# Linear attention followed by an MLP mixer on one core: loads of one batch placed anew, small matmuls regrouped, u transposed by slabs, and the last tile split

## The chip, the core and the metric

The kernel runs on one core of a Trainium2 chip. The time is the device time in microseconds of one execution; before the change it was 253.14 us (median of three runs, 253.03 to 253.78). The profile is of one more execution, with a span of 251.7 us.

## The reference

```python
# q, k, v: (8 batches, 8 heads, 576 positions, 64), float32; phi(x) = elu(x) + 1
kv  = einsum('bhsd,bhse->bhde', phi(k), v);  z = sum(phi(k), axis=2)
x   = (phi(q) @ kv) / (phi(q) . z + 1e-6)         # heads side by side: (8, 576, 512)
u   = x + (relu(x^T @ w_tok1) @ w_tok2)^T         # tokens: 576 -> 256 -> 576
out = u + relu(u @ w_ch1) @ w_ch2                 # channels: 512 -> 1536 -> 512
```

## The kernel before, in words

**Tiling.** Each batch has 576 positions: four tiles of 128 and a tail of 64. The tails of two batches (0 and 1, 2 and 3, ...) are put together into one tile of 128, `ut`. Matmuls are in bf16 and accumulate in eight PSUM banks.

**Stages of one batch n.** `load` (L126) brings q, k and v in halves c = 0 and 1 from SyncE's queue into `raw`; batch 1 has buffers of its own, all others share one set. `phi_exp` (ScalarE), `phi_add` and `phi_end` (VectorE, L151 to L164) make phi of k and q; `vcast` (L171) casts v to `vs` in halves, which `kv` (L181) multiplies with phi(k) in 64x64 tiles of TensorE, half 0 and then half 1; two ScalarE copies (L194) put the result into `kvbd`. `qtr_dma` (L216) transposes phi(q) by DMA. `nd` or `nd_all` (L249) multiplies by `kvbd` and divides: that is x. `mm1` (L296) and `mm2` (L307) are the token MLP and give u; `mm2_tails` (L330) does the tail rows of two batches in 128x64 tiles of TensorE and adds x to them on VectorE (L340), which gives `ut`. u is transposed, by DMA (`utr_dma` L508, `utr_tail_dma` L514) for batches 2 to 7, by TensorE for batches 0 and 1 (`utr_first` L487, `utr` L362), where PSUM is then copied into `uT` by ScalarE and VectorE. `mm3` (L520) is the first channel matmul, twelve groups of four matmuls of 512 columns (`mm3(n, mc, range(0, 2))` does half of a group), with the relu into `cr` on ScalarE or VectorE; `mm3_tail` (L537) is the same for the tails' tile, in three parts.

**The second channel matmul.** For batches 1 to 7 it is done in seven block products (`pair_product` L679, and `product` L629 for batch 7) instead of eight. `row_sums` (L620) prepares their left sides. The products 1, 6, 7 and 4 accumulate onto one bank X in this order, with readings in between: `pair_copy` (ScalarE) and `pair_end` (L699, VectorE adds u; GpSimd then adds a copied part at L703). A product that accumulates onto a bank has to wait until the reading ahead of it is done. The tails' tile goes through `mm4(p, 8, ...)` (L548) in full.

**Order.** It is written out by hand. TensorE runs a list of large pieces `big` (in batch n's block: twelve mm3 groups, three tail groups when n is odd, fourteen products, and the three parts of the tails' tile when n is odd). `fill` is a list of (step, piece) pairs: a piece is emitted after the large piece with that number. In the blocks from batch 2 on (L978 to L1042), `b0` is the step of the first product (12 or 15), and the fill pieces work on batches n+1 and n+2: `nd`, `mm1`, `mm2` and the transposes of u of batch n+1, `phi`, `vcast` and `kv` of batch n+2, loads of batch n+3. Each engine takes its instructions in the order in which they are emitted, SyncE's queue of transfers too. What stands behind a waiting instruction in such a queue waits with it.

**Places that the change touches.** The start of batch 0 (L833 to L840, and `big` at L893); casts and `kv` of batch 1 (`late`, L904); the block of batch 1 (L921 to L976) with `kv` of batch 2 at step 8, `nd` of batch 2 at step 10, `qtr_dma(3)` at step 15, the transposes of u of batch 2 at steps 19 and 24, and all loads of batch 4 (q, v, k) at step 25; the blocks of batches 2 to 6, with `mm2_tails` and its transpose `utt` at step b0 + 6, loads of q and v at b0 + 7, and `kv` and then `pair_end` X at b0 + 9; the order `LAST` (L709) of batch 7.

Of the kernel before, what the change touches and what calls it, by code (L numbers as in the profile page):

```python
# [10 lines left out]
BF16 = mybir.dt.bfloat16  # L11
# [7 lines left out]
def kernel(  # L19
# [20 lines left out]
    nc = tc.nc  # L40
# [5 lines left out]
    R = 4  # L46
# [6 lines left out]
    NDM = DM // 128  # L53
    NCH = DCH // 128
# [10 lines left out]
    def bank(at=None):  # L65
        if at is None:
            at, ring[1] = ring[1], (ring[1] + 1) % 4
        return psum[:, at]
# [6 lines left out]
    def two16():  # L75
        return banks().bitcast(BF16).rearrange("p a (t s) -> p a t s", s=128)


    def const(name, shape, dt=BF16):
        return consts.tile(shape, dt, name=name, tag=name)  # L80
# [17 lines left out]
    u = [const(f"u{b}", [128, R, DM]) for b in range(2)]  # L98
    ut = [const(f"ut{i}", [128, DM]) for i in range(2)]
    uT = [const(f"uT{b}", [128, R, NDM, 128]) for b in range(2)]  # L100
    uTt = const("uTt", [128, NDM, 128])
    cr = [const(f"cr{b}", [128, NCH, SM]) for b in range(2)]
    crt = const("crt", [128, NCH, 128])
# [19 lines left out]
    def rb(n):  # L123
        return 1 if n == 1 else 0
# [46 lines left out]
    def vcast(n, c, copy=nc.scalar.copy):  # L171
        js = slice(2 * c, 2 * c + 2)
        copy(out=vs[:, js, :, 0:D],  # L173
             in_=raw["v", rb(n)][:, js].rearrange("p j (t d) -> p j t d", t=T))
# [187 lines left out]
    def utr(n, js):  # L362
        b = n % 2
        for jp in js:
            tp = bank(4 + 2 * jp).bitcast(BF16).rearrange("p (j r c) -> p j r c", j=2, r=R)
            for i in range(2):
                j = 2 * jp + i
                for r in range(R):
                    nc.tensor.transpose(out=tp[:, i, r, :],
                                        in_=u[b][:, r, 128 * j:128 * j + 128], identity=identity)  # L370
            for i, copy in enumerate((nc.scalar.copy, nc.vector.tensor_copy)):
                copy(out=uT[b][:, :, 2 * jp + i], in_=tp[:, i])

    COLS = [slice(0, DM // 2), slice(DM // 2, DM)]

# [111 lines left out]
    def utr_first(js, put):  # L487
        tp = two16()[:, 0].rearrange(
            "p (j r) c -> p j r c", j=2)[:, 0:len(js)]
        for i, j in enumerate(js):  # L490
            for r in range(R):
                nc.tensor.transpose(out=tp[:, i, r, :],
                                    in_=u[0][:, r, 128 * j:128 * j + 128], identity=identity)
        put(out=uT[0][:, :, js[0]:js[-1] + 1].transpose([0, 2, 1, 3]), in_=tp)

    def w2_put(kt, t0, t1):
        nc.gpsimd.tensor_copy(
# [22 lines left out]
    def mm3(n, mc, kjs=range(NDM), dve=False):  # L520
        b = n % 2
        if kjs[0] == 0:
            part_of[mc] = bank(None if n == 0 else (
                (0, 1, 0, 1, 2, 3, 0, 1, 2, 3, 0, 1) if n > 1 else
                (3, 5, 7, 0, 3, 1, 2, 0, 3, 1, 0, 1))[mc])
        ps = part_of[mc]
        for kj in kjs:
            nc.tensor.matmul(out=ps, lhsT=wc1[:, kj, 128 * mc:128 * mc + 128],  # L528
                             rhs=uT[b][:, :, kj],
                             start=(kj == 0), stop=(kj == NDM - 1))  # L530
        if kjs[-1] == NDM - 1 and dve:
            nc.vector.tensor_scalar(out=cr[b][:, mc, :], in0=ps, scalar1=0.0, scalar2=None,
                                    op0=ALU.max)
        elif kjs[-1] == NDM - 1:
            nc.scalar.activation(out=cr[b][:, mc, :], in_=ps, func=AF.Relu)  # L535
# [169 lines left out]
    def pair_put(n):  # L705
        for e in range(2):
            nc.gpsimd.dma_start(out=outv[n, :, e:e + 7:2], in_=live["o4"][half[e]])

    LAST = [(1, 0), (2, 0), (6, 0), (5, 0), (7, 0), (3, 0), (4, 0), None,  # L709
            (1, 1), (2, 1), (6, 1), (5, 1), (7, 1), (3, 1), (4, 1)]  # L710

    def m4s(n):
        if n + 1 < B:
            return [lambda i=i, j=j: pair_product(n, i, j) for i in ORDER for j in range(2)]
        out_ = []
        for e in LAST:
            out_ += [lambda e=e: product(n, e[1], e[0])] if e else m4(n // 2, [8])
        return out_

    def prep_k(n, g, copy=nc.scalar.copy):  # L720
        phi("k", n, g)
# [69 lines left out]
    dve, act = nc.vector.tensor_copy, nc.scalar.copy  # L791
# [45 lines left out]
        mm3(0, mc, range(0, 2))  # L837
    utr_first([2], act)
    utr_first([3], dve)
    mm3(0, 2, range(0, 2))  # L840

    for nm in "kqv":
        for c in range(2):
# [28 lines left out]
    def run(bigs, fill):  # L872
# [5 lines left out]
        for s, fn in fill:  # L878
# [4 lines left out]
    m4 = lambda p, ts: [lambda t=t, i=i: mm4(p, t, range(4 * i, 4 * i + 4))  # L883
                        for t in ts for i in range(3)]


    def m4_0(kc):
        ts, kcs = (range(2 * kc, 2 * kc + 2), [0, 1]) if kc < 2 else (range(R), [kc])
        for k_ in kcs:
            for t in ts:  # L890
                mm4(0, t, [k_], wait=True)

    big = [lambda mc=mc: mm3(0, mc, range(2, 4)) for mc in range(3)] + \  # L893
        [lambda mc=mc: mm3(0, mc, dve=mc in (3, 6, 9)) for mc in range(3, NCH)] + \
        [lambda kc=kc: m4_0(kc) for kc in range(NCH)]
    at0 = {"qt0": 12, "qt1": 14, "vc": 13, "kv": 14, "nd00": 15, "nd01": 16, "nd10": 17,
           "nd11": 18, "nd20": 19, "nd21": 20, "mm1": 21}
# [1 line left out]
    for ex, ad, en, nm, c in ((2, 2, 3, "k", 0), (5, 5, 6, "k", 1), (8, 8, 9, "q", 0),  # L899
# [1 line left out]
        fill += [(ex, lambda nm=nm, c=c: phi_exp(nm, 1, 2 * c, 2)),  # L901
                 (ad, lambda nm=nm, c=c: phi_add(nm, 1, 2 * c, 2)),
                 (en, lambda nm=nm, c=c: phi_end(nm, 1, 2 * c, 2))]
    late = [("vc", lambda: vcast(1, 0)), ("vc", lambda: vcast(1, 1, nc.vector.tensor_copy))]  # L904
    fill += [(21, lambda g=g: phi("q", 2, g)) for g in range(2)]
    fill += [(22, lambda: qtr_dma(2)), (22, lambda: load_all(3, "q"))]
    fill += [(22, lambda: weight_sums((tf, B12, B11), (tb[1], B22, tf)))]
# [10 lines left out]
    for mc in range(3):  # L918
        mm3(1, mc, range(0, 2))
    utr_tail(0)  # L920
    big = [lambda mc=mc: mm3(1, mc, range(2, 4)) for mc in range(3)] + [  # L921
        lambda mc=mc: mm3(1, mc, dve=mc in (5, 8)) for mc in range(3, NCH)] + [
        lambda i=i: mm3_tail(i, False) for i in range(3)] + m4s(1) + m4(0, [8])
    fill = []
    put = lambda s, fn, *a: fill.append((s, lambda: fn(*a)))
# [11 lines left out]
    put(4, vcast, 2, 0)  # L937
    put(5, vcast, 2, 1, nc.vector.tensor_copy)
    put(6, load_all, 3, "v")
    put(8, kv, 2, range(2))  # L940
    for g in range(2):
        put(9, phi_add, "q", 3, 2 * g, 2)
    put(10, todo["nd"])
# [24 lines left out]
    put(24, pair_end, 1, "Z", 0, 0, 0)  # L968
    put(24, todo["mm2b"])
    put(24, todo["utb"])  # L970
    put(25, load_all, 4, "qvk")
    put(26, pair_end, 1, "Y", 0, 1, 1)
    put(28, pair_end, 1, "X", 1, 0)
    put(28, pair_put, 1)
# [3 lines left out]
    for n in range(2, B - 1):  # L978
        p, b = divmod(n, 2)
        big = m3(n) + (m3t if b else []) + m4s(n) + (m4(p, [8]) if b else [])  # L980
        b0 = 15 if b else 12
        todo = dict(steps(n + 1))
        fill = []
        put = lambda s, fn, *a: fill.append((s, lambda: fn(*a)))
        at = lambda s, *nms: [put(s, todo.pop(nm)) for nm in nms if nm in todo]

        def phi_at(nm, ex, ad, en):
            for g in range(2):
                if ex is not None:
                    put(ex[g], phi_exp, nm, n + 2, 2 * g, 2)  # L990
            for g in range(2):
                put(ad[g], phi_add, nm, n + 2, 2 * g, 2)
                put(en[g], phi_end, nm, n + 2, 2 * g, 2)

        at(1, "nd")
        if n + 2 < B:
            if n > 3:
                phi_at("k", None, (2, 2), (3, 4))
                put(5, load_all, n + 3, "k")
            if n != 3:  # L1000
                phi_at("q", (7, 7), (8, 9), (9, 10))
            else:
                phi_at("k", (7, 7), (8, 9), (9, 10))
            put(10, *((qtr_dma, n + 2) if n != 3 else (load_all, n + 3, "k")))
            if n == 2:
                for g in range(2):
                    put(10, phi_add, "k", n + 2, 2 * g, 2)
        at(7, "mm1")
        for s, k0 in ((11, 0), (12, 3)):
            for w in (1, 2):  # L1010
                put(s, row_sums, n, w, k0, 3)
        if n == 3:
            phi_at("q", (12, 13), (13, 13), (14, 14))
            put(15, qtr_dma, n + 2)
        at(13, "mm2a", "uta")
        put(14, row_sums, n, 3, 0, KH)
        put(b0 + 1, pair_copy, 0)
        if n == 2:
            for g in range(2):
                put(b0 + 1, phi_exp, "k", n + 2, 2 * g, 2)  # L1020
                put(b0 + 2, phi_end, "k", n + 2, 2 * g, 2)
            put(b0 + 4, load_all, n + 3, "k")
        at(b0 + 3 - b, "mm2b", "utb")
        put(b0 + 4 - b, row_sums, n, 4, 0, KH)
        put(b0 + 4 - b, pair_end, n, "Z", 0, 0, 0)
        put(b0 + 5, pair_copy, 1)
        if n + 2 < B:
            for g in range(2):
                put(b0 + (5 if n == 2 else 2) + g, vcast, n + 2, g)
        at(b0 + 6, "mm2t", "utt")  # L1030
        put(b0 + 7, load_all, n + 3, "qv")
        put(b0 + 7, pair_copy, 2)
        if n > 2 and n + 3 < B:
            put(b0 + 8, k_exp, n + 3)
        if n + 2 < B:
            put(b0 + 9, kv, n + 2, range(2))
        put(b0 + 9, pair_end, n, "X", 1, 1, 2)
        put(b0 + 11, pair_end, n, "Y", 0, 1, 1)
        put(b0 + 13, pair_end, n, "X", 1, 0)
        put(b0 + 13, pair_put, n)  # L1040
        assert not todo, todo
        run(big, sorted(fill, key=lambda e: e[0]))  # L1042

    n = B - 1
# [33 lines left out]
```

## Time and profile before

| | |
|---|---|
| median time | 253.14 us |
| span of the profiled run | 251.7 us |
| TensorE matmuls | 240.4 us busy, 2411 |
| VectorE | 171.3 us busy, 296 |
| ScalarE | 141.0 us busy, 224 |
| GpSimd | 68.8 us busy, 80 |
| granted TensorE clock | 0.997 |
| DMA | 48.39 MB, mean 192 GB/s |

A page of the profile has busy times, a strip of 40 slices of the span, the queues of DMA, the chain of work that ended last, and the costliest groups of instructions. A group stands as line, engine, operation, written tile <- read tiles, shape and count. In the timeline each row begins with the start and the duration, both in us, and ends, in brackets, with the idle time of the engine just before and what ended it. Neighbouring instructions of one kind are merged into one row; its count is behind the x. A few matmul records are missing from the trace, so that a count can be one short. "PE" is the matmul side of TensorE, "PEld" its weight load; "SPq" is the queue of SyncE from which transfers are issued.

### The profile page before, as it was taken

How to read it: one execution, taken by the hardware profiler on the slowest of the kernel's cores; microseconds unless marked ns; L12 is line 12 of the kernel's file. 1: busy time of each engine (PE TensorE's matmuls, PEld its weight loads, DVE VectorE, ACT ScalarE, POOL GpSimd, SP SyncE). 2: the span in 40 equal slices, each digit the busy share in tenths (PEclk: the TensorE clock that was granted, in tenths of full speed). 3: DMA queues.
4: the chain of work that ended last, by engine and by line, in shares of the span. 5: the costliest groups of instructions: out<-in, count | busy, mean ns of one | idle time of the engine just before them, and what ended most of it. 6: DMA issues, size and time to landing. Idle time of an engine off the chain costs nothing.

```text
span 251.7 us, 5859 instructions
## 1 busy us (share of the span) xinstructions
PE 240.4 (96%) x2411; PEld 151.6 (60%) x2430; DVE 171.3 (68%) x296; ACT 141.0 (56%) x224; POOL 68.8 (27%) x80
## 2 busy tenths in 40 slices
PE   7699999999999999989999999999999999999993
PEld 3584455554867546754578545774678445764962
DVE  5955777889998466967594397939863444834542
ACT  4764781578774378626896178556863265137300
POOL 9770130496703500061004500250004500260000
PEclk9999999999999999999999999999999999999998
DMA  6999999999534999389938956569142540435034
GB/s 239 261 203 262 347 257 339 322 274 294 233 51 87 227 399 261 69 225 392 348 76 196 393 153 219 120 208 353 45 97 46 112 99 0 83 66 124 0 97 115
DMA packets 49707, 48.39 MB, mean 192 GB/s; under 512 B 30032, under 2 KB 35536, under 8 KB 49680
## 3 DMA queue, kind: packets, MB, share of 16 engines
q1 hardware_dynamic: 41568, 34.87, 46.5%
q0 software_dynamic: 7568, 12.49, 22.0%
q10 hardware_dynamic: 544, 0.66, 1.1%
q8 instruction: 19, 0.31, 0.5%
q14 instruction: 8, 0.07, 0.1%
HBM read 35.85 MB, written 9.44 MB: 180 GB/s over the span
## 4 chain that ended last, share of the span: by engine, by line
PE 76%; DVE 8%; DMA 7%; ACT 4%; issue 2%; SPq 1%; DVEq 0%; ACTq 0%
PE ps L528 25%; PE ps L692 19%; DMA k_raw<-in_k_dram 7%; PE ps L555 6%; PE ps L302 5%; PE ps L542 4%; PE ps L643 4%; PE ps L315 3%; PE ps L188 2%; PE ps L258 1%; DVE kp L162 1%; ACT e L148 1%; DVE y L154 1%; DVE v_raw L625 1%; PE ps L463 1%
## 5 line engine op out<-in xcount | busy, mean ns | idle before, releaser
L528 PE MATMUL ps<-uT,wc 128*128 128x512 bf16 x384 | 87.2, 379 | 0.0
L535 ACT ACTIVATE cr<-ps 128x512 bf16<-128x512 f32 x91 | 53.2, 600 | 43.7 <-PE ps L528 43.3
L528 PEld LDWEIGHTS <-wc 128*128 128x128 bf16 x384 | 36.7, 98 | 43.4 <-issue 1.4
L703 POOL TENSOR_TENSOR obuf<-obuf,q_raw 128x512 f32<-128x512 f32 x6 | 7.6, 1263 | 98.3 <-ACT w L697 76.8
L625 DVE TENSOR_TENSOR v_raw<-cr 128x768 bf16<-128x768 bf16 (+1 forms) x21 | 14.4, 687 | 16.2 <-ACT cr L535 16.2
L701 DVE TENSOR_TENSOR obuf<-ps,u 128x512 f32<-128x512 f32 x24 | 16.3, 688 | 13.4 <-PE ps L692 8.6
L692 PE MATMUL ps<-k_raw,v_raw 128*128 128x256 bf16 x216 | 25.2, 273 | 0.0
L692 PEld LDWEIGHTS <-cr 128*128 128x128 bf16 x216 | 21.0, 98 | 5.6 <-issue 1.3
L692 PEld LDWEIGHTS <-v_raw 128*128 128x128 bf16 x216 | 20.9, 98 | 4.5 <-issue 1.2
L148 ACT ACTIVATE e<-q_raw 128x1152 bf16<-128x1152 f32 x16 | 18.3, 1160 | 6.9 <-DMA q_raw<-in_q_dram 6.3
L148 ACT ACTIVATE e<-k_raw 128x1152 bf16<-128x1152 f32 x16 | 18.2, 1163 | 4.0 <-DMA k_raw<-in_k_dram 3.9
L692 PE MATMUL ps<-wc,cr 128*128 128x256 bf16 x144 | 17.7, 273 | 0.0
L271 DVE TENSOR_TENSOR x<-ps,dens 128x768 bf16<-128x768 f32 x18 | 17.2, 958 | 0.6
L327 DVE TENSOR_TENSOR u<-ps,x 128x1024 bf16<-128x1024 f32 x12 | 14.7, 1221 | 3.5 <-PE ps L315 3.3
L154 DVE TENSOR_SCALAR y<-k_raw 128x1152 bf16<-128x1152 f32 x16 | 11.7, 754 | 4.9 <-DMA k_raw<-in_k_dram 4.9
L162 DVE TENSOR_TENSOR kp<-e,y 128x1152 bf16<-128x1152 bf16 x16 | 11.8, 751 | 3.5 <-ACT e L148 3.4
L162 DVE TENSOR_TENSOR qp<-e,y 128x1152 bf16<-128x1152 bf16 x16 | 11.9, 756 | 3.3 <-ACT e L148 2.5
L302 PE MATMUL ps<-x,w 128*128 128x512 bf16 x49 | 13.8, 379 | 0.3
L154 DVE TENSOR_SCALAR y<-q_raw 128x1152 bf16<-128x1152 f32 x16 | 13.7, 867 | 0.0
L173 ACT CAST vs<-v_raw 128x1152 bf16<-128x1152 f32 x12 | 13.5, 1163 | 0.0
L703 POOL TENSOR_TENSOR obuf<-obuf,part 128x512 f32<-128x512 f32 x6 | 7.6, 1268 | 18.1 <-DVE obuf L701 18.1
L542 PEld LDWEIGHTS <-wc 128*128 128x128 bf16 x192 | 11.3, 98 | 1.5
(132 smaller groups left out, 348.5 us busy)
## 6 DMA issues: line engine op xcount, KB each, us to landing
k_raw<-in_k_dram SPq DMA_DIRECT2D x16, 576.0 KB, 6.3
q_raw<-in_q_dram SPq DMA_DIRECT2D x16, 576.0 KB, 6.1
v_raw<-in_v_dram SPq DMA_DIRECT2D x14, 576.0 KB, 9.8
out_dram<-obuf POOLq DMA_DIRECT2D x12, 512.0 KB, 7.0
wc<-in_moe_w_ch_dram POOLq DMA_DIRECT2D x8, 384.0 KB, 10.2
out_dram<-obuf POOLq DMA_DIRECT2D x4, 256.0 KB, 5.2
out_dram<-obuf POOLq DMA_DIRECT2D x6, 128.0 KB, 6.7
cr<-in_v_dram POOLq DMA_DIRECT2D x2, 288.0 KB, 7.6
```

What stands on the lines that cost most here:

```text
L148: nc.scalar.activation(out=e, in_=f, func=AF.Exp)
L154: nc.vector.tensor_scalar(out=y, in0=f, scalar1=1.0, scalar2=1.0, op0=ALU.add, op1=ALU.max)
L162: live["phi"] = nc.vector.tensor_tensor(out=dst.transpose([0, 2, 1, 3]), in0=e.rearrange("p (i t d) -> p i t d", i=nj, t=T), in1=y.rearran ...
L271: nc.vector.tensor_tensor(out=xv[:, :, rc0:rc0 + 3], in0=v_[:, :, k0:k0 + 6, 0:D].rearrange("p i (q a) d -> p i q a d", a=2), in1=den[:, : ...
L302: nc.tensor.matmul(out=ps[:, mt], lhsT=w1t[:, b, ms] if r == R else w1[:, r, ms], rhs=x[b][:, r, :], start=(r == 0), stop=(r == R))
L528: nc.tensor.matmul(out=ps, lhsT=wc1[:, kj, 128 * mc:128 * mc + 128], rhs=uT[b][:, :, kj], start=(kj == 0), stop=(kj == NDM - 1))
L535: nc.scalar.activation(out=cr[b][:, mc, :], in_=ps, func=AF.Relu)
L542: nc.tensor.matmul(out=ps[:, m], lhsT=wc1[:, kj, 128 * mc:128 * mc + 128], rhs=uTt[:, kj, :], start=(kj == 0), stop=(kj == NDM - 1))
L625: nc.vector.tensor_tensor(out=sb[which - 1][:, ks], in0=x_, in1=y_, op=op)
L692: nc.tensor.matmul(out=live[tile_][:, j], lhsT=lhs[:, k_], rhs=rhs[:, k_], start=(first and j == 0 and k_ == 0), stop=(k_ == KH - 1), skip ...
L701: nc.vector.tensor_tensor(out=o, in0=live[tile_], in1=u[n % 2][:, d::2, HC[c]], op=ALU.add)
L703: nc.gpsimd.tensor_tensor(out=o, in0=o, in1=part[i], op=ALU.add)
```

## The change

1. **Loads of batch 4.** q is issued at step 16 of batch 1's block instead of step 25, and k comes ahead of v.
2. **mm2 of the tails next to kv.** In the blocks of batches 2, 4 and 6 `mm2_tails` moves from b0 + 6 to b0 + 9, directly ahead of `kv`, and its transpose behind `kv`. `pair_end` X at the same step is now emitted ahead of both.
3. **Casts and kv of batches 1 and 2.** For batch 1 VectorE casts the half of v that `kv` reads first, ScalarE the other. `kv` of batch 2 moves from step 8 to 9.
4. **Slabs of transposed u for batches 0 and 1.** `uTj` is the same memory as `uT`, with the order j, r, c instead of r, j, c, so that what one copy writes and one matmul reads is contiguous. In `utr` the two copies get a bank each, and VectorE takes the first.
5. **Start.** The first half of the mm3 group 3 of batch 0 is done ahead of the second halves.
6. **Last batch.** The three parts of the tails' tile, which stood together in the middle, are put between products, and the products of the two column halves are interleaved.

It is meant to shorten the waits of TensorE, the queue of VectorE and the changes between tilings of TensorE.

```diff
+    uTj = [t.rearrange("p r j c -> p (r j c)").rearrange("p (j r c) -> p j r c", j=NDM, r=R) for t in uT]
...
-            tp = bank(4 + 2 * jp).bitcast(BF16).rearrange("p (j r c) -> p j r c", j=2, r=R)
+            tp = [bank(4 + 2 * jp + i).bitcast(BF16)[:, 0:512].rearrange("p (r c) -> p r c", r=R)
+                  for i in range(2)]
...
-            for i, copy in enumerate((nc.scalar.copy, nc.vector.tensor_copy)):
-                copy(out=uT[b][:, :, 2 * jp + i], in_=tp[:, i])
+            for i, copy in enumerate((nc.vector.tensor_copy, nc.scalar.copy)):
+                copy(out=uTj[b][:, 2 * jp + i], in_=tp[i])
...
-        put(out=uT[0][:, :, js[0]:js[-1] + 1].transpose([0, 2, 1, 3]), in_=tp)
+        put(out=uTj[0][:, js[0]:js[-1] + 1], in_=tp)
...
-                             rhs=uT[b][:, :, kj],
+                             rhs=uTj[b][:, kj] if n < 2 else uT[b][:, :, kj],
...
-    LAST = [(1, 0), (2, 0), (6, 0), (5, 0), (7, 0), (3, 0), (4, 0), None,
-            (1, 1), (2, 1), (6, 1), (5, 1), (7, 1), (3, 1), (4, 1)]
+    LAST = [(1, 0), (2, 0), 0, (6, 0), (5, 0), 1, (7, 0), (1, 1), 2, (3, 0), (2, 1), (4, 0),
+            (6, 1), (5, 1), (7, 1), (3, 1), (4, 1)]
...
-    mm3(0, 2, range(0, 2))
+    for mc in range(2, 4):
+        mm3(0, mc, range(0, 2))
...
-    big = [lambda mc=mc: mm3(0, mc, range(2, 4)) for mc in range(3)] + \
-        [lambda mc=mc: mm3(0, mc, dve=mc in (3, 6, 9)) for mc in range(3, NCH)] + \
+    big = [lambda mc=mc: mm3(0, mc, range(2, 4), dve=mc == 3) for mc in range(4)] + \
+        [lambda mc=mc: mm3(0, mc, dve=mc in (6, 9)) for mc in range(4, NCH)] + \
...
-    late = [("vc", lambda: vcast(1, 0)), ("vc", lambda: vcast(1, 1, nc.vector.tensor_copy))]
+    late = [("vc", lambda: vcast(1, 0, nc.vector.tensor_copy)), ("vc", lambda: vcast(1, 1))]
...
-    put(8, kv, 2, range(2))
+    put(9, kv, 2, range(2))
...
-    put(25, load_all, 4, "qvk")
+    put(16, load_all, 4, "q")
+    put(25, load_all, 4, "kv")
...
-        at(b0 + 6, "mm2t", "utt")
...
+        put(b0 + 9, pair_end, n, "X", 1, 1, 2)
+        at(b0 + 9, "mm2t")
         if n + 2 < B:
             put(b0 + 9, kv, n + 2, range(2))
-        put(b0 + 9, pair_end, n, "X", 1, 1, 2)
+        at(b0 + 9, "utt")
```

More of the change, by code (lines that the diff above doesn't have):

```diff
@@ L368, in utr @@
                 for r in range(R):
-                    nc.tensor.transpose(out=tp[:, i, r, :],
+                    nc.tensor.transpose(out=tp[i][:, r, :],
                                         in_=u[b][:, r, 128 * j:128 * j + 128], identity=identity)
-            for i, copy in enumerate((nc.scalar.copy, nc.vector.tensor_copy)):
-                copy(out=uT[b][:, :, 2 * jp + i], in_=tp[:, i])
+            for i, copy in enumerate((nc.vector.tensor_copy, nc.scalar.copy)):
+                copy(out=uTj[b][:, 2 * jp + i], in_=tp[i])
     COLS = [slice(0, DM // 2), slice(DM // 2, DM)]
@@ L714, in m4s @@
             return [lambda i=i, j=j: pair_product(n, i, j) for i in ORDER for j in range(2)]
[L715 to L718, printed above, removed]
+        tails = m4(n // 2, [8])
+        return [(lambda e=e: product(n, e[1], e[0])) if isinstance(e, tuple) else tails[e]
+                for e in LAST]
     def prep_k(n, g, copy=nc.scalar.copy):
```

## The prediction

> **What bounds the kernel.** I read the page first (busy time, then the chain of work that ended last), then TensorE's own waits, then the timeline around each of them.
>
> ```profile
> PE 240.4 (96%) x2411; PEld 151.6 (60%) x2430; DVE 171.3 (68%) x296; ACT 141.0 (56%) x224; POOL 68.8 (27%) x80
> ...
> PE 76%; DVE 8%; DMA 7%; ACT 4%; issue 2%; SPq 1%; DVEq 0%; ACTq 0%
> ```
>
> TensorE is busy for 96% of the span and carries 76% of the chain. The change adds no matmul and takes none away, so it can only pay by closing gaps between matmuls. The waits of TensorE name the three large ones after the start:
>
> ```profile
> PE ps L692 <- DVE obuf L701: 1.1, 1, 1.1
> ...
> PE ps L188 <- ACT vs L173: 0.4, 1, 0.4
> PE ps L188 <- DVE vs L173: 0.3, 1, 0.3
> ```
>
> *The largest*, in the block of batch 2. Timeline (start, duration, engine, line, operation; in brackets the idle time before):
>
> ```profile
> 84.47 1.32 SPq L129 DMA_DIRECT2D k_raw<-in_k_dram  x2
> ...
> 97.50 0.76 DVE L154 TENSOR_SCALAR y<-k_raw 128x1152 bf16<-128x1152 f32 x1 [1.41 <-DMA k_raw<-in_k_dram]
> ...
> 99.01 0.76 DVE L154 TENSOR_SCALAR y<-k_raw 128x1152 bf16<-128x1152 f32 x1 [0.74 <-DMA k_raw<-in_k_dram]
> ...
> 107.14 0.68 DVE L701 TENSOR_TENSOR obuf<-ps,u 128x512 f32<-128x512 f32 x1
> ...
> 107.74 1.38 DVE L340 TENSOR_TENSOR ut<-ps,x 64x512 bf16<-64x512 f32 x2
> ...
> 109.15 1.29 DVE L701 TENSOR_TENSOR obuf<-ps,u 128x512 f32<-128x512 f32 x2
> ...
> 109.89 1.47 PE L692 MATMUL ps<-q_raw,cr 128*128 128x256 bf16 x12 [1.13 <-DVE obuf L701]
> ```
>
> Read upwards: product 4 accumulates onto bank X and must wait until `pair_end` X (the first of the two at 109.15) has read it. VectorE got there late, because the two `ut` additions stood ahead of it (1.38 us) and because its queue had stood still for k of batch 4 (1.41 + 0.74 us), the last loaded of q, v, k.
>
> *kv of batch 1* is next: it wants both halves of `vs`, and the half that is read first is the one ScalarE makes last.
>
> ```profile
> 35.01 0.76 DVE L173 CAST vs<-v_raw 128x1152 bf16<-128x1152 f32 x1
> ...
> 35.22 1.20 ACT L173 CAST vs<-v_raw 128x1152 bf16<-128x1152 f32 x1
> ...
> 36.47 0.78 PE L188 MATMUL ps<-vs,kp 64*64 64x65 bf16 x72 [0.45 <-ACT vs L173]
> ```
>
> *kv of batch 2* stops in its middle for the half cast by VectorE:
>
> ```profile
> 59.67 1.40 DVE L173 CAST vs<-v_raw 128x1152 bf16<-128x1152 f32 x1
> ...
> 61.12 0.48 PE L188 MATMUL ps<-vs,kp 64*64 64x65 bf16 x36 [0.34 <-DVE vs L173]
> ```
>
> *The transposed u of batch 1* is copied out of one bank by two engines in turn; VectorE waits for ScalarE:
>
> ```profile
> 51.81 0.42 DVE L372 COPY uT<-ps 128x512 bf16<-128x512 bf16 x1 [0.30 <-ACT uT L372]
> ```
>
> *The last batch*: 18 matmuls of three products take 0.08 us longer than 18 of them in the block of batch 4, since a product waits for VectorE's read of the tile that it accumulates onto:
>
> ```profile
> 236.91 2.21 PE L643 MATMUL ps<-k_raw,v_raw 128*128 128x256 bf16 x18
> ```
>
> ```profile
> 159.23 2.13 PE L692 MATMUL ps<-k_raw,v_raw 128*128 128x256 bf16 x18
> ```
>
> **What the Trainium skill says.** (1) "TensorEngine Tiling (Array Packing)", Key Properties: changing the tiling mode drains TensorE. The trace agrees: 18 matmuls of 0.109 us from 159.23 end at 161.20, `mm2_tails` starts at 161.29, its two pairs of 0.216 us end at 161.72, and the next product starts at 161.84: 0.09 in, 0.12 out. (2) "PSUM — Partial Sum Buffer", PSUM bank collisions raise a hardware error: accesses of two engines are to be kept apart by bank, two readers included. The 0.30 us wait above is that order. (3) "SBUF — State Buffer", SBUF: two separate sides: VectorE's two-port operations and GpSimd lock one another out. The cast of `vs` took 0.76 us with GpSimd idle and 1.40 us beside L611 on GpSimd; it agrees. (4) "DMA: Bandwidth & Descriptors", Queues, rings and completion order: each DMA engine takes descriptors in ring order. Loads issued from 82.31 on in the order q, v, k were waited for at 97.5 and 99.0 for k; it agrees.
>
> **The change part by part.**
>
> *Loads of batch 4.* q moves to step 16 of batch 1's block (about 72 to 75 us; window 69 to 84 has a DMA share of 0.45 and 79 GB/s, so there is room), k comes ahead of v. The buffers are free: q of batch 3 was last read at 69.3. k then is first at about 82.3 and lands 6.3 us later (the median of the page) to 13.8 us later (the k load in the chain): 89 to 96. VectorE wants it after qp at 96.1, so the 1.41 + 0.74 us vanish. Behind the earlier q in the ring stands the transpose of the first half of u, issued at 76.47 and needed at 84.19: up to 4 us late costs nothing. The second half goes out at 81, when 1.15 MB of q have passed.
>
> *`mm2_tails` next to kv, `pair_end` X ahead of it.* VectorE now does X before the `ut` additions: from 107.82 at the latest, done 108.5, while product 4 could begin at 107.28 + 12 x 0.109 + pipeline, at 108.6 to 108.8. With k early it is done about 1.5 us before. Either edit closes the gap; together they gain it once: **1.19 us** (109.89 minus the end of product 3's twelve matmuls, 107.28 + 1.31 = 108.59, less 0.11 that I keep back as the dependency's own latency). Mode changes: one exit and one entry (0.12 + 0.10) become one change between the two tilings, which the trace has nowhere; it costs 0 to 0.12. I take 0.12: gain 0.10 in the blocks of batches 2 and 4, **0.2**; in batch 6's there is no kv: 0. New wait: the transpose of the tails (`utt`) now stands behind the q and v loads of batch 5 in SyncE's queue. 3.46 MB from 106 on, at the pace of 82.3 to 99 (also 3.46 MB, 16.7 us), end at 122.7 at worst, some 115 at the 400 GB/s that the page shows in its best slices; plus 2.5 us to landing gives 117.5 to 125. `mm3_tail` wants it at 124.55, less what TensorE has gained, about 122.2. I take no wait; the worst case is 3 us in this block.
>
> *kv of batch 1.* VectorE makes the half read first, done 35.77. TensorE's nine transposes from 35.36 end at 35.87 (0.056 each), mode change 0.09: kv starts at 35.96, its first half takes 0.35, then it waits for ScalarE's half (36.42) until 36.47 and needs 0.35 more: end 36.82 instead of 37.18. **0.35.** nd then needs `kvbd` (two ScalarE copies of 0.38): they move with kv.
>
> *kv of batch 2* four matmuls later. 60.30 to 61.54 is 1.24 us against 0.72 at 106.56 to 107.28: 0.52 lost, closed by the 0.86 us that now lie ahead of it. But only one mm3 group (0.86) is left between kv and nd, and `kvbd` is ready 0.24 + 0.77 = 1.01 after kv: a new wait of 0.1. **0.4.** VectorE is busy 14.79 of 15.00 us in window 54 to 69, so it could become the limit at `mm1` (69.04, its inputs done 68.77); it starts that stretch 0.38 earlier because of the next edit, so I let the gain stand.
>
> *Slabs.* For batch 1 each copy has its own bank: VectorE starts at 51.50 when its previous addition ends. mm3's gap (six matmuls in 1.62 against 1.30 + 0.16 of pipeline) shrinks from 0.16 to 0.06: **0.1**. mm3 group 2 uses bank 7, now read by ScalarE until 52.6; it starts at 52.8: no wait. Contiguous slabs for the matmul: 0, since 36 matmuls of batch 0 on the strided tile already run at 0.216 each.
>
> *Fourth mm3 half early*: fills 0.18 (eight matmuls in 2.07 us against 1.73 + 0.16), but at 33.12 TensorE waits for VectorE's qp, which hangs on k of batch 1 landing at 29.03. TensorE would wait there for what it gained. **0.**
>
> *Last batch.* Each wait of a product for VectorE's read (starts in the timeline less the matmuls ahead at 0.109 us: 0.07 + 0.10 + 0.03 in the first column half, 0.08 in the second) gets a tails part of 4 x 0.216 us or another product in between: **0.25**. The 512 KB of output that left at 240.96 now leave at about 244.7, near the last pieces; the page gives 3.3 to 4.0 us to landing, so 248.7, ahead of the final piece (issued about 248, landed 250). I charge 0.05.
>
> Sum: 1.19 + 0.2 + 0.35 + 0.4 + 0.1 + 0.25 - 0.05 = 2.44. Time 253.14 - 2.44 = **250.7 us**.
>
> **Rivals.** (a) *Only the large gap closes.* The small gains run into VectorE at `mm1` and into ScalarE around 58.5, where a 0.15 us gap stands behind relus that follow one another without pause: 1.19 + 0.1 = 1.3, **251.8 us**. For it: two engines near their limit in 54 to 69. Against: both start that stretch earlier. (b) *The gap stays in part*, because kv and `mm2_tails` delay ScalarE or VectorE elsewhere: 0.5 gained, **252.6 us**. Against: in the blocks of batches 4 and 6 the same queues leave no gap. (c) *Transfers collide, slower.* If plain loads hold up the transposes, the second half of u comes late at 84.19 (slack about 0.1): 3.4 us at worst for q's 1.15 MB at the pace seen, and `mm3_tail` waits up to 3 us; 253.14 - 2.44 + 3.4 = **254.1 us** with the first alone. For it: ring order. Against: 6 us lie between q's issue and that transpose.
>
> **Numbers.** Forecast 0.72, (a) 0.18, (b) 0.05, (c) 0.05. Faster by over 0.3% (below 252.38): forecast and (a), 0.90; within: 0.05; slower: 0.05. The range takes the forecast with its bounds down to 250.1 (mode change free: 0.24; `kvbd` wait 0; all of the batch 1 gap; the fill at the start) and reaches past (a), 252.0.
>
> **What would show it.** Right: no wait of L692 for L701 near 108; VectorE's y of k without a DMA wait near 96; kv of batch 1 starting about 0.5 us earlier; one stretch of L336 then L188 in two blocks; last matmul near 245.3 instead of 247.6. Wrong: a wait of L542 for the DMA of `uTt`, of L528 for `uT` at 84, of L258 for `kvbd` above 0.3, or of L302 for x near 69.

## The result and the profile after

The changed kernel took 251.19 us (median of four executions, 250.99 to 251.63) against 253.2 us (median of four executions of the kernel before): a ratio of 0.9919, 95% interval 0.9898 to 0.994, or 2.0 us less (1.5 to 2.6). Run again in two later sets it took 252.84 us (14 executions, ratio 0.9981, 0.9958 to 1.0005) and 251.81 us (5 executions, 0.9934, 0.9918 to 0.9951). A sixth execution of the last set, 255.85 us at a granted clock of 0.993, was in a slow state and is left out here and below. All three sets point the same way, but the interval of the second reaches 1, so that the size is less clear than the direction: single executions reached from 251.0 to 254.8, and what is known of the reason is taken up below. Line numbers of the changed kernel are one or two higher than before.

First the page, in the same two lines:

```profile
PE 240.6 (97%) x2430; PEld 151.9 (61%) x2430; DVE 171.3 (69%) x296; ACT 141.2 (57%) x224; POOL 68.4 (27%) x80
...
PE 84%; DMA 11%; POOL 3%; issue 0%; SPq 0%; DVE 0%; POOLq 0%
```

TensorE does the same work in a span of 249.2 us instead of 251.7. VectorE and ScalarE have left the chain but for one addition of 0.42 us at its end. What is left beside TensorE is DMA and GpSimd, and the chain in order of time shows that these are all ahead of 36.7 us: the start now hangs on weights, the second quarter of w_ch2 (start, duration, what):

```profile
18.86 11.14 DMA q_raw<-in_q_dram
...
30.54 6.10 DMA wc<-in_moe_w_ch_dram
...
36.68 1.02 PE ps L557 x4
```

TensorE's waits. The three of before (L692, and L188 twice) are gone; the first two new rows are L544 (`mm3_tail`) and L557 (`mm4`):

```profile
PE ps L544 <- DVE x L279: 0.4, 1, 0.4
...
PE ps L557 <- DMA wc<-in_moe_w_ch_dram: 0.3, 1, 0.3
```

The place of the largest wait, in the timeline:

```profile
95.21 1.42 DVE L155 TENSOR_SCALAR y<-k_raw 128x1152 bf16<-128x1152 f32 x2
...
105.10 0.62 PE L337 MATMUL ps<-ar,w2p 128*64 128x512 bf16 x4
105.66 0.78 PE L189 MATMUL ps<-vs,kp 64*64 64x65 bf16 x72
...
107.69 1.47 PE L694 MATMUL ps<-q_raw,cr 128*128 128x256 bf16 x12
```

VectorE takes k of batch 4 without a wait, tails and kv follow one another, and product 4 has no bracket: it follows product 3 at once.

Where the 2.44 us of the two profiled spans went is read from the starts of a few matmuls (first matmul of `mm1` of batches 1 to 6, first product of batch 7, last matmul, end), as lengths between them in us:

| stretch | before | after | difference |
|---|---|---|---|
| start to mm1 of batch 1 | 44.48 | 43.90 | -0.58 |
| to mm1 of batch 2 | 24.56 | 24.33 | -0.23 |
| to mm1 of batch 3 | 22.88 | 22.89 | +0.01 |
| to mm1 of batch 4 (the large wait) | 27.02 | 25.61 | -1.41 |
| to mm1 of batch 5 | 30.33 | 30.33 | 0.00 |
| to mm1 of batch 6 | 25.72 | 25.62 | -0.10 |
| to the first product of batch 7 | 60.54 | 60.53 | -0.01 |
| to the last matmul | 11.95 | 11.69 | -0.26 |
| to the end | 4.18 | 4.31 | +0.14 |

### The profile page after: what moved, and what is told of

Read it like the earlier page. It is cut to its first block, busy times and chain, and to the rows that moved or that the text cites. A ratio compares the mean times of both kernels' runs of the same rounds, so it can differ in the third digit from the quotient of the medians.

```text
span 249.2 us, 5887 instructions
## 1 busy us (share of the span) xinstructions
PE 240.6 (97%) x2430; PEld 151.9 (61%) x2430; DVE 171.3 (69%) x296; ACT 141.2 (57%) x224; POOL 68.4 (27%) x80
## 4 chain that ended last, share of the span: by engine, by line
PE 84%; DMA 11%; POOL 3%; issue 0%; SPq 0%; DVE 0%; POOLq 0%
PE ps L530 29%; PE ps L694 22%; PE ps L557 7%; DMA wc<-in_moe_w_ch_dram 6%; PE ps L303 6%; DMA q_raw<-in_q_dram 4%; PE ps L544 4%; PE ps L316 4%; PE ps L645 4%; PE ps L259 2%; PE ps L189 2%; POOL qT L761 1%; PE ps L355 1%; PE ps L337 1%; POOL cr L135 1%; PE ps L230 0%
## 5 line engine op out<-in xcount | busy, mean ns | idle before, releaser
L694 PE MATMUL ps<-k_raw,v_raw 128*128 128x256 bf16 x216 | 24.7, 273 | 0.0
L303 PE MATMUL ps<-x,w 128*128 128x512 bf16 x56 | 14.4, 379 | 0.0
L316 PE MATMUL ps<-ar,w2p 128*128 128x512 bf16 x50 | 12.9, 379 | 0.0
L544 PEld LDWEIGHTS <-wc 128*128 128x128 bf16 x192 | 11.3, 98 | 1.9 <-issue 0.5
```

Of the source, the lines that this page charges most:

```text
L303: nc.tensor.matmul(out=ps[:, mt], lhsT=w1t[:, b, ms] if r == R else w1[:, r, ms], rhs=x[b][:, r, :], start=(r == 0), stop=(r == R))
L316: nc.tensor.matmul(out=ps[:, i], lhsT=w2v(kt, r, b), rhs=ar[b][:, kt, :], start=(kt == 0), stop=(kt == NT - 1 and not add))
L544: nc.tensor.matmul(out=ps[:, m], lhsT=wc1[:, kj, 128 * mc:128 * mc + 128], rhs=uTt[:, kj, :], start=(kj == 0), stop=(kj == NDM - 1))
L694: nc.tensor.matmul(out=live[tile_][:, j], lhsT=lhs[:, k_], rhs=rhs[:, k_], start=(first and j == 0 and k_ == 0), stop=(k_ == KH - 1), skip ...
```

## Experiments

Each set ran on one chip beside the kernel before; its own timing is noisier than most of the effects, so the verdicts rest on these stretches and on waits, each read from one profiled execution, and the times are given beside them. Stretches that an edit doesn't touch agree within 0.02 us from one profile to the next; the start doesn't (43.90, 44.41 and 44.20 in the three profiles of the changed kernel), and why is shown under "The start".

### One half at a time: loads, tails, the rest

The loads alone:

```diff
-    put(25, load_all, 4, "qvk")
+    put(16, load_all, 4, "q")
+    put(25, load_all, 4, "kv")
```

> Kernel before with the loads of batch 4 placed anew and nothing else. Theory of the prediction (either edit alone closes the large gap, because VectorE comes out of its wait for k about 1.5 us earlier): the 1.13 us wait of product 4 in the block of batch 2 is gone, and the time is 1.2 us below the kernel before, about 252.0. Rival (the two ut additions ahead of pair_end X are the cause, and early data does not help): most of the wait stays, 0.5 us or more, and the time is at most 0.5 us below.

Measured: 252.48 us, ratio 0.9985 (0.9967 to 1.0003). The stretch to mm1 of batch 4 took 25.72 us, 1.30 less than before: the large wait is gone, as the prediction had it. But the stretch ahead of it took 23.47 us, 0.59 more. Timeline of this kernel:

```profile
76.19 1.13 SPq L129 DMA_DIRECT2D q_raw<-in_q_dram  x2
...
84.89 1.47 PE L528 MATMUL ps<-uT,wc 128*128 128x512 bf16 x6 [0.41 <-DMA uT<-u]
```

mm3 of batch 2 waits for the transposed u, which stands behind q's load. Of the 1.30 us that were won, 0.59 are given back one stretch earlier.

The tails alone: `mm2_tails` from b0 + 6 to b0 + 9 ahead of kv, `pair_end` X ahead of both, `utt` behind.

```diff
-        at(b0 + 6, "mm2t", "utt")
...
+        put(b0 + 9, pair_end, n, "X", 1, 1, 2)
+        at(b0 + 9, "mm2t")
         if n + 2 < B:
             put(b0 + 9, kv, n + 2, range(2))
-        put(b0 + 9, pair_end, n, "X", 1, 1, 2)
+        at(b0 + 9, "utt")
```

> Kernel before with mm2 of the tails next to kv and pair_end X ahead of both, and nothing else; q, v, k of batch 4 as before. Theory of the prediction: VectorE still waits for k of batch 4 (1.4 + 0.7 us), but pair_end X is done at about 108.5 and product 4 waits for less than 0.1 us; with two saved changes of tiling at 0.1 each the time is 1.4 us below the kernel before, about 251.8. Rival (the late k is the cause, the order of the ut additions does not matter): 0.5 us or more of the wait stays and the time is at most 0.7 us below.

Measured: 252.98 us, ratio 0.998 (0.9961 to 0.9998). Neither theory fits. Product 4 starts with no wait (the order of the additions does matter), yet the stretch to mm1 of batch 4 is only 0.35 us shorter (26.67):

```profile
105.09 1.22 DVE L327 TENSOR_TENSOR u<-ps,x 128x1024 bf16<-128x1024 f32 x1
...
111.09 1.90 PE L528 MATMUL ps<-uT,wc 128*128 128x512 bf16 x8 [0.85 <-DMA uT<-u]
```

k is still late, so VectorE is late with the second half of u of batch 3 (12.93 us after mm1 of that batch, against 11.33 in the changed kernel), its transpose is late, and the next mm3 waits for that. A second wait had stood behind the first. The stretch to mm1 of batch 6, which has no late load, is 25.61, against 25.72 before and in the kernel with the loads alone: 0.11 us is the saved change of tiling by itself.

Everything else without these two:

```diff
-    put(16, load_all, 4, "q")
-    put(25, load_all, 4, "kv")
+    put(25, load_all, 4, "qvk")
...
+        at(b0 + 6, "mm2t", "utt")
...
-        put(b0 + 9, pair_end, n, "X", 1, 1, 2)
-        at(b0 + 9, "mm2t")
...
-        at(b0 + 9, "utt")
+        put(b0 + 9, pair_end, n, "X", 1, 1, 2)
```

> The changed kernel with the old placing of the loads of batch 4 and the old place of mm2 of the tails; the casts, kv of batch 2, slabs, start and last batch as changed. Theory of the prediction: 0.35 + 0.4 + 0.1 + 0.2 = 1.05 us below the kernel before, about 252.1, with the 1.13 us wait of product 4 still there. Rival read from the trace after (kv of batch 2 gives back what it gained, when the second part of mm3_tail waits for VectorE's reading of nd): 0.6 to 0.7 below, about 252.5. In both the large wait stays between 0.7 and 1.3 us.

Measured: 252.5 us, ratio 0.9978 (0.9962 to 0.9993), nearer to the rival. The wait of product 4 is there (0.9 us in TensorE's waits). In this execution the start won nothing (44.59 to mm1 of batch 1), with the same code that won 0.58 in the first profile of the changed kernel. Nine profiles with the new start code give 43.90 to 44.68, mean 44.30; three with the old give 44.48 to 44.70, mean 44.60. The two ranges overlap, and three profiles are few; 0.3 us on average is what they show for the start, and the rest of the 0.58 is the execution. k of batch 1 doesn't explain it: it was worked on from 28.46 in that profile, and here, with no gain, from 28.51. What does is shown under "The start".

### kv of batch 2

```diff
-    put(9, kv, 2, range(2))
+    put(8, kv, 2, range(2))
```

> The changed kernel with kv of batch 2 back at step 8. Theory of the prediction: 0.4 us slower than the changed kernel, kv stopping in its middle for VectorE's cast again and mm1 of batch 2 about 0.4 us later. Rival read from the trace after: the wait in kv comes back (0.3 to 0.5 us) but the wait of the second part of mm3_tail for VectorE (0.37 us) goes, and mm1 of batch 2 starts within 0.1 us of where it does in the changed kernel; no difference in time that can be measured.

Measured: 251.59 us, ratio 0.9926 (0.9903 to 0.9949). The rival holds, by the stretches; the times can't tell, since the changed kernel itself gave 251.19, 252.84 and 251.81 us in its three sets. From the transposes of the tails (L506) to mm1 of batch 2 it takes 15.58 us with kv at step 8 and 15.60 at step 9. Timeline of the kernel with step 8:

```profile
60.44 0.48 PE L189 MATMUL ps<-vs,kp 64*64 64x65 bf16 x36 [0.26 <-DVE vs L174]
...
64.28 2.91 PE L544 MATMUL ps<-uTt,wc 128*128 128x128 bf16 x48
```

and of the changed kernel:

```profile
65.14 1.95 PE L544 MATMUL ps<-uTt,wc 128*128 128x128 bf16 x32 [0.37 <-DVE x L279]
```

The wait only moved: from inside kv to the second part of `mm3_tail`, which writes a bank that VectorE has still to read for x of batch 2.

### Where the load of q belongs

> The changed kernel once more, as the measure for the others of this set. Theory: the load of q of batch 4 at step 16 stands in SyncE's queue and in the rings between the transposes of phi(q) of batch 3 and of u of batch 2, so that in some executions TensorE waits up to 0.6 us for uT at about 84 us, as in the runs with only the loads changed (0.57) and with kv of batch 2 put back (0.56), and in others not, as in the first profile of the changed kernel. Expected time 251.2. Rival: that wait belongs to those two kernels alone, and the changed kernel never has it.

The changed kernel again: 252.84 us; in its profile mm3 of batch 2 starts 0.29 us later than the matmuls ahead of it ask for, so the wait is not those two kernels' alone. SyncE's queue in this execution, then in the first profile of the changed kernel:

```profile
72.00 3.67 SPq L219 DMA_TRANSPOSE qT<-qp  x2
75.77 1.40 SPq L130 DMA_DIRECT2D q_raw<-in_q_dram  x2
```

```profile
71.48 2.91 SPq L219 DMA_TRANSPOSE qT<-qp  x2
74.48 1.44 SPq L130 DMA_DIRECT2D q_raw<-in_q_dram  x2
```

The transposes ahead occupy the queue for 2.9 to 3.9 us, and q's load starts when they are through. Over all kernels that load q there, with the landings of q's second half and of the two halves of transposed u:

| q issued at, us | 74.48 | 74.93 | 75.42 | 75.77 | 75.91 | 76.19 |
|---|---|---|---|---|---|---|
| q landed | 81.15 | 81.51 | 81.83 | 82.23 | 82.05 | 82.59 |
| first half of uT landed | 82.17 | 82.54 | 82.90 | 83.24 | 83.11 | 83.75 |
| second half of uT landed | 83.30 | 83.66 | 84.01 | 84.14 | 84.22 | 84.85 |
| mm3 of batch 2 late by, us | 0 | 0.03 | 0.56 | 0.29 | 0.49 | 0.57 |

The landings show how. The first half of uT lands 1.0 to 1.2 us after q, the second 0.9 to 1.1 us after the first. The time from the issue of the first half to its landing, in the kernel before and then in the kernel with the loads alone (last number, us):

```profile
uT<-u SPq DMA_TRANSPOSE x1, 3.1
```

```profile
uT<-u SPq DMA_TRANSPOSE x1, 6.3
```

So the load holds up the first half by 3 us (6.0 to 6.3 in the six profiles, against 3.1). The first half has that time to spare; what reaches TensorE is the second half, which stands behind the first.

Loading q ahead of those transposes:

```diff
-    put(16, load_all, 4, "q")
+    put(14, load_all, 4, "q")
```

> The changed kernel with the load of q of batch 4 at step 14, so that it is issued ahead of the transposes of phi(q) of batch 3 (step 15), when its buffer is free (about 69 us). Theory: q's data pass at about 70.5 to 75, the transposes of u of batch 2 follow without it, and no wait of TensorE for uT is left at 84; 0.2 to 0.5 us below the changed kernel. Rival (the transposes, not q's load, hold each other up): the wait is there as before, no difference.

Measured: 251.22 us, ratio 0.9917 (0.9904 to 0.9931), four executions within 0.5 us. The load is issued at 66.58, the transposes of phi(q) again take 3.67 us, and mm3 of batch 2 starts on time:

```profile
66.58 1.91 SPq L130 DMA_DIRECT2D q_raw<-in_q_dram  x2
```

The opposite direction, between the two transposes of u:

```diff
-    put(16, load_all, 4, "q")
+    put(20, load_all, 4, "q")
```

> The changed kernel with the load of q of batch 4 between the transposes of the first and the second half of u of batch 2 (step 20) instead of ahead of both (step 16). Theory (ring order: a transpose behind 1.15 MB of plain load lands when the load has passed): load data from about 79 to 83, second half of uT at about 85, and a wait of TensorE for uT near 84 of 1 to 2 us; 1 to 1.5 us slower than the changed kernel without its wait. Rival (plain loads do not hold up the transposes): wait at most 0.6 us, as at step 16.

Measured: 251.88 us, ratio 0.9937 (0.9921 to 0.9952). mm3 of batch 2 is late by 0.61 us:

```profile
80.95 1.24 SPq L512 DMA_TRANSPOSE uT<-u  x1
...
84.76 1.47 PE L530 MATMUL ps<-uT,wc 128*128 128x512 bf16 x6 [0.45 <-DMA uT<-u]
```

The wait is as small as the rival has it, but the landings are those of the theory: q lands at 83.71, the second half of uT at 84.72, 1.0 us after q and 3.8 us after its own issue (3.1 to 3.2 in the kernels with q at step 14 or at step 25). The first half, now ahead of q, lands 3.2 us after its issue. The transpose does wait for the load; TensorE waits so little because the load had been issued 3.2 us ahead of the transpose.

> The changed kernel itself, beside the others of this set on one chip. Theory: a wait for uT at about 84 us of between 0 and 0.6 us from one execution to the next, so a median about 251.3 to 252.8 with a wider spread than with q at step 14 (251.0 to 251.5 in the set before). Rival: the wide spread of the set before was that chip's, and the spread here is as narrow as with q at step 14.

The third time, in a set on another chip: 251.81 us, 251.21 to 252.03, and in its profile, with q issued at 74.93, no wait for uT. The nineteen executions of four kernels with q at step 14 lie between 250.82 and 251.9; of the changed kernel's 23, nine lie above 252.1, all in its second set. This agrees with the load being the sensitive part, but it doesn't show it: a wait of 0.6 us doesn't explain 254, the six executions of the kernel with kv of batch 2 put back, which also loads q at step 16, stay below 251.9, and the kernel with the tails alone, which doesn't, reaches from 251.5 to 253.6. No profile shows one of the long executions; their cause stays open.

### VectorE in the block of batch 1, and a kernel that beats both

The kernel with q at step 14, and the two additions for phi(q) of batch 3 behind nd of batch 2:

```diff
+    put(10, todo["nd"])
     for g in range(2):
-        put(9, phi_add, "q", 3, 2 * g, 2)
-    put(10, todo["nd"])
+        put(10, phi_add, "q", 3, 2 * g, 2)
```

> As the run before it (q of batch 4 at step 14), and in addition the two additions of phi(q) of batch 3 on VectorE come behind nd of batch 2 (step 10) instead of ahead of it (step 9). Theory (the gain of moving kv of batch 2 was lost because VectorE, not TensorE, sets when the banks of nd come free for the second part of mm3_tail): the 0.37 us wait of mm3_tail for VectorE's x goes, the times of all later blocks are 0.4 us earlier, 0.4 to 0.8 us below the changed kernel in all, about 250.5. Rival: the wait turns up again at the block products (row_sums later) or at mm1, gain below 0.1.

Measured: 250.88 us (250.82 to 251.25), ratio 0.9906 (0.9893 to 0.9919), the fastest of all. The stretch to mm1 of batch 2 takes 23.81 us, 0.52 less than with q at step 14 alone. The 48 matmuls of `mm3_tail` now run through, and the two additions take 1.42 us instead of 2.76, since GpSimd's subtractions beside which they ran are over:

```profile
64.39 2.84 PE L544 MATMUL ps<-uTt,wc 128*128 128x128 bf16 x48
...
67.74 1.42 DVE L155 TENSOR_SCALAR y<-q_raw 128x1152 bf16<-128x1152 f32 x2
```

That is about what moving kv had been forecast to give, and could not. Of the 0.52 us, 0.18 go again in the next stretch, where mm3 of batch 2 waits for uT at 83.7: VectorE now comes later to u, and the second half of u is issued 12.13 us after mm1 of batch 2 instead of 11.95. This belongs to the edit, for the last kernel below, which has it too, shows the same. In the profiled execution TensorE also waits 0.5 us for w_ch2 near 37.

### The last batch

```diff
-    LAST = [(1, 0), (2, 0), 0, (6, 0), (5, 0), 1, (7, 0), (1, 1), 2, (3, 0), (2, 1), (4, 0),
-            (6, 1), (5, 1), (7, 1), (3, 1), (4, 1)]
+    LAST = [(1, 0), (2, 0), (6, 0), (5, 0), (7, 0), (3, 0), (4, 0), 0, 1, 2,
+            (1, 1), (2, 1), (6, 1), (5, 1), (7, 1), (3, 1), (4, 1)]
```

> The changed kernel with the old order of the last batch (seven products of one column half, the three parts of the tails' tile, seven products of the other). Theory of the prediction: four waits of products for VectorE's reads come back, together 0.25 to 0.33 us from the first of these products to the last matmul, and as much in the time. Rival: the wait moves to the outputs, whose last transfer ends the kernel, and the time from the last matmul to the end shrinks by as much; no difference in the span.

Measured: 252.02 us, ratio 0.9975 (0.9954 to 0.9996). From the first product of batch 7 to the last matmul it takes 11.95 us, as before the change, against 11.69; 18 matmuls need the 2.22 us again:

```profile
235.50 2.22 PE L645 MATMUL ps<-k_raw,v_raw 128*128 128x256 bf16 x18
```

From the last matmul to the end: 4.15 us here, 4.31, 4.30 and 4.19 in the three profiles of the changed kernel. So 0.26 us are won, and 0.04 to 0.16 are given back at the outputs.

### The start

Two parts taken back in the kernel with q at step 14: the old casts of v of batch 1, and the one bank for the two copies in `utr`.

```diff
-    late = [("vc", lambda: vcast(1, 0, nc.vector.tensor_copy)), ("vc", lambda: vcast(1, 1))]
+    late = [("vc", lambda: vcast(1, 0)), ("vc", lambda: vcast(1, 1, nc.vector.tensor_copy))]
...
-            for i, copy in enumerate((nc.vector.tensor_copy, nc.scalar.copy)):
-                copy(out=uTj[b][:, 2 * jp + i], in_=tp[i])
+            for i, copy in enumerate((nc.scalar.copy, nc.vector.tensor_copy)):
+                copy(out=uTj[b][:, 2 * jp + i], in_=tp[:, i])
```

> The changed kernel with q of batch 4 at step 14, and with two parts taken back: the casts of v of batch 1 (ScalarE the half read first) and the two copies of transposed u of batch 1 (one bank for both, ScalarE first; slabs stay contiguous). Theory of the prediction: from the end of TensorE's transposes near 35.8 to the first matmul after kv of batch 1 it takes 0.35 us longer, and the gap of 0.16 us in mm3 of batch 1 near 52 is back; 0.4 to 0.5 us slower than with q at step 14 alone. Rival (weights): TensorE already waits 0.2 to 0.5 us there for the second quarter of w_ch2, so that the old cast costs 0.1 us or nothing, and only the 0.16 us show; 0.1 to 0.3 us slower.

Measured: 251.73 us, ratio 0.9934 (0.9921 to 0.9948), against 251.22 with both parts (in a set on another chip). TensorE's transposes ahead of kv start at the same time in the two kernels (35.17 and 35.19), so the stretches compare:

```profile
36.28 0.78 PE L189 MATMUL ps<-vs,kp 64*64 64x65 bf16 x72 [0.45 <-ACT vs L174]
37.14 1.02 PE L556 MATMUL ps<-wc,cr 128*128 128x512 bf16 x4
```

The matmul behind kv starts at 37.14 instead of 36.78. Not all of this is the casts. Counted from the transposes, the last matmul of kv comes 0.29 us later; the rest is w_ch2, whose second quarter landed at 37.10 here and at 36.74 there, and in both kernels the matmul behind kv starts 0.04 us after that landing. mm3 at 52 has its gap of 0.16 again, and the stretch to mm1 of batch 2 takes 24.56 us, as before the change, against 24.33.

The weights explain the spread of the start. In the nine profiles with the new start code:

| second quarter of w_ch2 landed, us | 36.64 | 36.74 | 36.74 | 36.94 | 37.04 | 37.15 | 37.32 | 37.33 | 37.41 |
|---|---|---|---|---|---|---|---|---|---|
| mm1 of batch 1 starts, us | 43.90 | 44.01 | 44.03 | 44.20 | 44.30 | 44.41 | 44.58 | 44.59 | 44.68 |

mm1 starts 7.26 to 7.29 us after the landing in all nine, and the first column is the first profile of the changed kernel. In the profile before the change the weights landed at 36.9 and kv ended last, with mm1 7.55 us after them. So the new casts bring kv far enough forward for the weights to be what is left, and the landing sets how much of the gain shows.

The weights earlier, in the fastest kernel:

```diff
-    c2_in += [after(load_wc2(i), landed["q1", 0] if i == 1 else None) for i in range(1, NB)]
+    c2_in += [after(load_wc2(i), {1: landed["k1", 1], 2: landed["q1", 0]}.get(i)) for i in range(1, NB)]
...
-            load(nm, 2, c, c2_in[1] if nm == "q" and c == 0 else None)
+            load(nm, 2, c, c2_in[2] if nm == "q" and c == 0 else None)
```

> The kernel with q of batch 4 at step 14 and the additions of phi(q) of batch 3 behind nd, and in addition the second quarter of w_ch2 released by the landing of k of batch 1 (second half, about 28.7) instead of q of batch 1 (about 30.8); the third quarter is released by q of batch 1, and q of batch 2 by the third quarter. Theory (the gain of the new casts was cut by weights that land at about 36.7 to 37.4): the 0.5 us wait of TensorE for w_ch2 goes, 0.3 to 0.5 us faster than without this edit, about 250.5. Rival (q and v of batch 1 share the bandwidth and land later): TensorE waits as long for phi(q) or the casts of v, no gain or a loss of up to 0.5 us.

Measured: 251.32 us, ratio 0.9921 (0.9906 to 0.9935). The rival holds: the wait for w_ch2 is gone, but the weights take 7.4 us to land instead of 6.1 (at 36.74), v of batch 1 lands later, and mm1 of batch 1 starts at 44.59, as without the edit (44.58).

```profile
35.69 1.15 ACT L174 CAST vs<-v_raw 128x1152 bf16<-128x1152 f32 x1 [0.52 <-DMA v_raw<-in_v_dram]
...
36.89 0.48 PE L189 MATMUL ps<-vs,kp 64*64 64x65 bf16 x36 [0.65 <-ACT vs L174]
```

## Why the prediction was right, and where its steps were not

The forecast was 250.7 us, a gain of 2.44; measured was a gain of 2.0 (1.5 to 2.6), and 2.44 between the two profiled spans. That the sum fits the spans to the hundredth is luck: the start brought 0.58 where 0.35 was counted, because the weights landed early in that execution; the block of batch 1 brought 0.23 where 0.5 was counted, the large wait with the changes of tiling 1.51 where 1.39 was, the last batch 0.12 where 0.20 was. The main mechanism, product 4 waiting for VectorE and VectorE for k, was right. Step by step:

- *The large wait plus one change of tiling*, 1.29 predicted: 1.41 measured. Right in cause; the 0.11 us kept back as latency was gained too. "Either edit closes the gap" was true of the wait itself, with either edit alone, and wrong of the gain. With the tails alone the transposed u of batch 3 takes its place (0.85 us); the prediction followed the late k into `pair_end` but not into u and its transpose.
- *The change of tiling*, 0.10 per block: 0.10 and 0.11 measured in the block of batch 4, where nothing else changed.
- *kv of batch 1*, 0.35: kv itself ends 0.29 earlier. The forecast hadn't looked at when w_ch2 lands; the matmul behind kv waits for that in all nine profiles, so that of the start as a whole between 0.6 us and nothing could be seen.
- *Slabs*, 0.1: the whole gap of 0.16 closed, and the stretch to mm1 of batch 2 became 0.23 shorter. The two banks with VectorE first do it: with one bank and ScalarE first, and the slabs still contiguous, the stretch is 24.56 again, so that contiguity shows no gain, as forecast.
- *kv of batch 2*, 0.4: none that the run with step 8 can show. The failed step is "I let the gain stand". VectorE had been named as near its limit, but only `mm1` was considered as the place where it would show; the waiting instruction was `mm3_tail`, for a bank and not for data. The 0.1 us wait for `kvbd` did not show: nd started 0.10 behind the matmul ahead of it, which is the change of tiling alone.
- *Fourth mm3 half early*, 0: it was not run by itself, and since the weights set when mm1 of batch 1 starts, no run here shows what it is worth.
- *Last batch*, 0.25 less 0.05: 0.26 less 0.04 to 0.16.
- *Loads of batch 4*: that k comes in time was right. "The second half goes out at 81, when 1.15 MB of q have passed" failed. The forecast had q issued at about 72 to 75; the queue of SyncE, held by the transposes ahead, released it at 74.5 to 76.2, and it took 6.1 to 6.7 us more to land, at 81.2 to 82.6. The first half of u came some 3 us late, within the 4 us that the forecast had found free for it; the second half stood behind it, and TensorE waited 0.3 to 0.6 us in four of six profiles. This is rival (c): the delay of a transpose came in nearly full size (3 us, against 3.4 feared), but on the half that had time to spare, so that TensorE felt at most about a sixth of it. From which pace the 3.4 us come, the prediction doesn't say. The feared wait of `mm3_tail` for `utt` never came: in the first profile the transposed tails landed at 121.89, within the forecast's 117.5 to 125, but only 0.45 us ahead of their use.
- *Rival (a)* named the right engine for the loss (VectorE between 54 and 69) and the wrong place.

## What to carry to other kernels

Behind a wait on the busiest engine there is often a second one, a little shorter, with the same root: ask what else the late engine makes late, transposes and their transfers included, before counting a wait as won. When a piece is moved to spare one wait, list for each following piece both its data and its banks, and who has still to read them. Put a load into a shared queue behind nothing that can hold it, and ahead of no transfer that is needed before the load can have landed: where it is issued is set by the instructions ahead of it in that queue, not by the step at which it is written, and what is issued behind it may land behind it.

## What the runs showed of the hardware

The two issues of a DMA transpose of phi(q) held SyncE's queue for 2.9 to 3.9 us, and for 2.9, 3.1 and 3.7 us in three profiles of one kernel; why is open. A transpose issued behind a plain load of 1.15 MB in that queue landed after the load in every profile that has this order: the first half of u 1.0 to 1.2 us after q and 6.0 to 6.3 us after its own issue, against 3.1 with no load ahead. From a 128x64 tiling straight to 64x64 (105.10 to 105.66, of which 0.45 are the matmuls) costs 0.10 us, about as much as from 128x128 to 64x64 (0.09, ahead of 163.91 in the kernel before). The changes of tiling seen here cost about the same, so that what saved time was to make one fewer.
